# 28 transposes of the identity on TensorE ahead of the first tile, in a one-core DFT and soft mixture-of-experts kernel

## The chip, the cores and the metric

The kernel runs on one core of one Trainium2 chip. The metric is the device time in microseconds (us) of one execution. It is measured in several runs and given as their median; one further execution is recorded by the hardware profiler, and its trace is what the rows below come from. A core has five engines that run side by side and wait for each other by semaphores: TensorE (PE; its weight loads are listed apart as PEld), VectorE (DVE), ScalarE (ACT), GpSimd (POOL) and SyncE (SP), which issues the DMA transfers here.

## The reference

A real input `x` of 8 x 2496 x 256 goes through a two-dimensional Fourier transform per batch entry, of which the real part is kept. The result, as 19968 tokens of 256 values, goes through a soft mixture of experts with 8 experts of 4 slots each.

```python
X = np.fft.fft(np.fft.fft(x, axis=1), axis=2).real      # (8, 2496, 256)
X = X.reshape(8 * 2496, 256)
logits = X @ phi                                        # phi: (256, 32)
d = softmax(logits, axis=0)                             # over all tokens
slot_input = (d.T @ X).reshape(8, 4, 256)
for e in range(8):
    slot_out[e] = np.maximum(slot_input[e] @ w1[e], 0) @ w2[e]
c = softmax(logits, axis=1)                             # over the 32 slots
out = c @ slot_out.reshape(32, 256)
```

## The kernel before, in words

The batch is cut into four pairs of entries, p = 0 to 3, and each pair into five tiles of `x`, t = 0 to 4. Every tile (up to 1 MB) is loaded by SP into a ring of six buffers, in the order of the list `LD`, which also places the tables `cs0` to `cs3` and `phi`. `cs0` holds nothing but the 128 x 128 identity, named `ident`; it is the first load of all.

A hand-written list, `ORDER`, names the parts of the program. For a tile, `part_a` adds mirrored rows of `x` on DVE (lines 220 and 222), folds the columns into a tile `eo` with one addition and one subtraction (224 and 225), turns `eo` in eight transposes on PE into two banks `pt` (229) and copies them to `et` on ACT (230). `part_z` multiplies two tiles' `et` by `wphi` (244), the transformed `phi`, which is made once from `psphi` (lines 187 to 193). `part_t`, `part_b` and `part_c` finish the logits of a pair (`zt`, `a`, `lp`, `lm`, `lt`) and find maxima (`mx`, `mt`, `mall`, `mex`, `nm`) and exponentials (`d`, `dpm`). `part_e`, `part_d` and `part_u` (335, 353, 376) carry the weights back and sum the pair's tokens: `u0` reads the folded tiles `eo` of pair 0. Fifteen buffers hold `eo`, so the fold of pair 3 (225 and 224 for `eo3_0` and on) needs those that `u0` has read. After all four pairs come the experts (`part_l`, line 477, `part_v`, 497) and the output (`part_o`, 608 to 621).

`ORDER` is the order in which the program is recorded. The order in which each engine runs it is decided by the build's scheduler, which may move instructions of neighbouring parts past each other; each engine then runs its own list strictly in that order. PSUM banks come from pools: `bank1` (two buffers, `pt` and `z`), `bank` (two) and `bank3` (three, `mt`, `e`, `d`, `tok`).

Of the kernel before, what the change touches and what calls it, by code (L numbers as in the profile page):

```python
# [25 lines left out]
CT = ['sa', 'lt', 'lt', 'lt']  # L26
LATE = 'zs'
SEB = 2
DE = 2
FIRST = [0, 1]  # L30
GATE = {0: ['u', 'acc', 'acc'], 1: ['rep', 'rep', 'rep']}
# [81 lines left out]
def _build(nc, tc, xh, phih, w1h, w2h, cins, where, out, out0):  # L113
    from contextlib import ExitStack, nullcontext

    v, sc, pe = nc.vector, nc.scalar, nc.tensor
    ctx = ExitStack()
    with ctx:
# [11 lines left out]
        def se(shape, name, dt=F32):  # L130
            return sb.tile(shape, dt, name=name, tag="se", bufs=SEB)

# [6 lines left out]
        def bufs_(tag):  # L139
            return {"zs": 2, "sa": 2, "se": SEB, "lt": LT}[tag]  # L140

# [3 lines left out]
        def bank3(name, dt=F32):  # L145
            return pp.tile([128, 512], dt, name=name, tag="ps3", bufs=P3)
# [28 lines left out]
        def C(name):  # L175
            i, o, r, w = where[name]
            return cs[i][:r, o : o + w]

        ident = C("ident")


        wphi = cp.tile([128, 3, NSLOT], F32, name="wphi")
# [164 lines left out]
        def part_d(p, hf):  # L347
            if hf == 0:
                dsb[p] = se([128, 2, NKC, NSLOT], f"ds{p}")
            for k in range(2):  # L350
# [7 lines left out]
                dst = dsb[p][:, k, :, 16 * hf : 16 * hf + 16]  # L358
                (v.tensor_copy if DE >> k & 1 else sc.copy)(dst, ps[:, :320].rearrange("p (s c) -> p c s", c=NKC))  # L359

# [334 lines left out]
```

## Time and profile before

| | |
|---|---|
| median of 3 runs | 195.04 us (194.52, 195.04, 195.69) |
| the profiled execution | 194.9 us |
| its span, first to last instruction | 193.0 us |
| PE busy in the span | 169.5 us (88%) |
| DVE, ACT, POOL busy | 125.2, 111.0, 20.9 us |
| mean granted TensorE clock in the records | 0.991 |

The 1.9 us between 194.9 and 193.0 lie outside the first and the last instruction. Busy shares are averages over stages with different limits; PE's busy time is modelled from the pipelined starts of its instructions. In a row of the trace, times are us from the start of the span; `x8` is the number of instructions that a row merges; in brackets stands how long the engine sat idle before the row and what ended the wait. Lines (L229) are those of the kernel before.

### The profile page before, as it was taken

The numbers are of one execution on the slowest core, as the hardware profiler recorded it, in microseconds if no ns is written. First come the engines' busy times: TensorE is split into PE (matmuls) and PEld (weight loads), VectorE is DVE, ScalarE is ACT, GpSimd is POOL, SyncE is SP. The second block draws the span as 40 slices with busy tenths as digits, with TensorE's granted clock in tenths as the row PEclk, the third lists the DMA queues.
The fourth block names the chain that finished last, engine by engine and source line by source line (L and its number), as shares of the span: only waits on it lengthen the run. The fifth ranks groups of instructions, "written<-read, shape, count | busy, mean of one in ns | idle before, by whom it ended". The sixth has DMA issues, their size and how long they took to land.

```text
span 193.0 us, 4197 instructions
## 1 busy us (share of the span) xinstructions
PE 169.5 (88%) x1682; PEld 107.7 (56%) x1682; DVE 125.2 (65%) x227; ACT 111.0 (58%) x244; POOL 20.9 (11%) x25
## 2 busy tenths in 40 slices
PE   0389899899999989999998999999998998988930
PEld 0376576577776866576863877256535443434400
DVE  0599877999995990832267553750489776985740
ACT  2132586587966485574862842521878595774630
POOL 0000000000000000000000000550055325522000
PEclk9999999999999999999999999999999999999996
DMA  5999999999980399600860689990279999999995
GB/s 170 415 428 410 420 419 418 425 417 418 385 297 5 112 362 430 289 3 20 285 242 3 226 317 285 410 393 13 92 292 418 392 409 411 351 409 402 415 433 222
DMA packets 10706, 59.16 MB, mean 307 GB/s; under 512 B 1344, under 2 KB 1728, under 8 KB 5696
## 3 DMA queue, kind: packets, MB, share of 16 engines
q1 hardware_dynamic: 10688, 58.91, 77.1%
q8 instruction: 13, 0.21, 0.4%
q14 instruction: 5, 0.04, 0.1%
HBM read 38.46 MB, written 20.45 MB: 305 GB/s over the span
## 4 chain that ended last, share of the span: by engine, by line
PE 79%; DVE 7%; ACT 5%; DMA 3%; issue 1%; POOL 1%; SPq 0%; ACTq 0%; DVEq 0%; POOLq 0%
PE po L608 18%; PE pt L229 10%; PE z L244 8%; PE e L335 7%; PE d L353 5%; PE a L279 5%; PE u L376 4%; PE h L477 4%; PE so L497 4%; PE lT L589 3%; DMA x<-xh 3%; PE lp L297 2%; PE lm L298 2%; PE cT L530 2%; PE zt L265 2%; ACT et L230 2%
## 5 line engine op out<-in xcount | busy, mean ns | idle before, releaser
L608 PE MATMUL po<-rh,lTs 64*128 64x512 f32 x160 | 38.1, 607 | 2.2 <-ACT lTs L592 2.1
L616 DVE COPY o<-po 128x512 f32<-128x512 f32 (+1 forms) x40 | 26.7, 681 | 17.5 <-PE po L608 17.1
L229 PE MATMUL pt<-cs,eo 128*128 128x128 f32 x160 | 26.3, 301 | 7.9 <-DVE eo L224 7.8
L230 ACT COPY et<-pt 128x512 f32<-128x512 f32 x40 | 22.8, 587 | 14.6 <-PE pt L229 14.6
L616 ACT COPY o<-po 128x512 f32<-128x512 f32 x40 | 23.2, 588 | 12.1 <-PE po L608 12.1
L229 PEld LDWEIGHTS pt<-cs,eo 128*128 128x128 f32 x160 | 19.8, 153 | 14.4 <-DVE eo L224 7.8
L608 PEld LDWEIGHTS po<-rh,lTs 64*128 64x128 f32 x160 | 14.3, 186 | 17.0 <-issue 10.2
L222 DVE TENSOR_TENSOR x<-x 128x1024 f32<-128x1024 f32 x16 | 19.4, 1217 | 2.9 <-DMA x<-xh 2.9
L244 PE MATMUL z<-et,wphi 128*32 128x256 f32 (+1 forms) x288 | 16.8, 368 | 2.3 <-ACT et L230 2.3
L547 POOL TENSOR_TENSOR c<-c,cm 128x640 f32<-128x640 f32 x8 | 10.0, 1266 | 68.4 <-DVE cm L546 68.4
L320 ACT ACTIVATE d<-lt,nm 120x128 f32<-120x128 f32 x44 | 13.7, 394 | 3.6 <-DVE nm L317 3.6
L335 PE MATMUL e<-cs,dpm 120*64 120x120 f32 x176 | 14.0, 273 | 0.0
L224 DVE TENSOR_TENSOR eo<-x 128x512 f32<-128x512 f32 x20 | 13.6, 682 | 0.3
L225 DVE TENSOR_TENSOR eo<-x 128x512 f32<-128x512 f32 x20 | 13.6, 680 | 0.0
L244 PEld LDWEIGHTS z<-et,wphi 128*32 128x32 f32 x288 | 8.1, 114 | 9.2 <-ACT et L230 3.8
L335 PEld LDWEIGHTS e<-cs,dpm 120*64 120x64 f32 x176 | 11.4, 136 | 2.4 <-issue 1.8
L279 PE MATMUL a<-cs,zt 128*120 128x128 f32 x88 | 11.8, 279 | 1.0 <-DVE lt L302 0.9
L252 ACT COPY zs<-z 128x512 f32<-128x512 f32 (+1 forms) x12 | 6.2, 514 | 10.4 <-PE z L244 10.4
L557 POOL TENSOR_TENSOR c<-c,cm 128x640 f32<-128x640 f32 x8 | 10.1, 1265 | 15.0 <-DVE cm L556 11.2
L376 PE MATMUL u<-eo,ds 128*32 128x129 f32 x320 | 11.5, 275 | 0.1
L279 PEld LDWEIGHTS a<-cs,zt 128*120 128x120 f32 x88 | 10.4, 183 | 2.1 <-DVE lt L302 1.1
L353 PE MATMUL d<-e,cs 128*64 128x320 f32 x64 | 10.7, 443 | 0.5 <-ACT ds L359 0.5
(91 smaller groups left out, 217.9 us busy)
## 6 DMA issues: line engine op xcount, KB each, us to landing
x<-xh SPq DMA_DIRECT2D x16, 1024.0 KB, 12.2
out<-o SPq DMA_DIRECT2D x15, 1024.0 KB, 5.2
w<-w1h SPq DMA_DIRECT2D x6, 1024.0 KB, 8.1
w<-w2h SPq DMA_DIRECT2D x12, 512.0 KB, 6.4
x<-xh SPq DMA_DIRECT2D x4, 896.0 KB, 12.0
out<-o SPq DMA_DIRECT2D x4, 768.0 KB, 5.1
w<-w1h SPq DMA_DIRECT2D x4, 512.0 KB, 5.7
w<-w2h SPq DMA_DIRECT2D x2, 1024.0 KB, 8.1
```

What stands on the lines that cost most here:

```text
L222: v.tensor_tensor(x[:, 0:4], x[:, 0:4], x[:, 4:8], op=ALU.add)
L224: v.tensor_tensor(e[:, :, 0:128], x[:, 0:4, 0:128], x[:, 0:4, 128:256], op=ALU.add)
L229: pe.transpose(b[:, g * 128 : g * 128 + 128], e[:, g, k * 128 : k * 128 + 128], ident)
L230: sc.copy(tr[k][:, :, :, qi, :], b.rearrange("p (g h a) -> p g h a", g=4, h=2))
L244: pe.matmul(z[32 * g : 32 * g + 32, o : o + n], wphi[:, w, :], tr[k][:, g].rearrange("p h q a -> p (h q a)"), start=w != 0, stop=w != 1, t ...
L279: pe.matmul(ps[:120, i * 128 : i * 128 + 128], zt[p][:, GS * g : GS * g + GS].rearrange("p s h c -> p (s h c)"), C("wa"), start=True, stop ...
L320: sc.activation(d[:, g], L[:, g], AF.Exp, bias=nm[:, g : g + 1], scale=1.0)
L335: pe.matmul(ps[64 * k : 64 * k + 64, 120 * i : 120 * i + 120], dpm[p, hf][:, k, 3 * j + i, :], C(name), start=True, stop=True, tile_positi ...
L353: pe.matmul(ps[64 * h : 64 * h + 64, :320], C("wb")[:, 64 * k : 64 * k + 64], esb[p].rearrange("p g (s h c) -> p (g s) h c", h=2, c=NKC)[: ...
L376: last = pe.matmul(ub[32 * g : 32 * g + 32, 0:129], dsb[p][:, k, c, :], e[:, 0:129] if k == 0 else e[:, 127:256], start=cc == 0, stop=cc == 9,
L608: ins = pe.matmul(po[h], lts[p, b, t][rows], rh[0][rows].rearrange("p k d -> p (k d)"), start=True, stop=True, tile_position=(64 * h, 0),)
L616: ins = ev(ot[:np_, 2 * i : 2 * i + 2, :].rearrange("p k d -> p (k d)"), po[h][:np_])
```

## The change

After the tables are named, one tile `warm` is taken from the pool `bank3`, and PE transposes the identity into it 28 times, over its four quarters in turn. Nothing reads `warm`. The only thing that the 28 instructions need is `cs0`.

```diff
+WARM = 28
 ...
         ident = C("ident")
 
 
+        warm = bank3("warm")
+        for i in range(WARM):
+            pe.transpose(warm[:, 128 * (i % 4) : 128 * (i % 4) + 128], ident, ident)
+
+
         wphi = cp.tile([128, 3, NSLOT], F32, name="wphi")
         ps = bank("psphi")
```

Each line number behind the change is higher by 6 (L229 becomes L235). The build's scheduler also orders other instructions differently. SP's and POOL's orders are as before. PE's, DVE's and ACT's differ between the first tile and the last pair's `u`, and agree from there on, but for three swaps on DVE in the output.

The first place is the start of the program. PE's list in the kernel before (an operand's last number is a running one, and `pt0_1_0` is pair 0, tile 1, half 0):

```order
L229 MATMUL pt0_0_0_150<-cs0_70,eo0_0_140 128x128 x4
L229 MATMUL pt0_0_1_156<-cs0_70,eo0_0_140 128x128 x4
L187 MATMUL psphi_101<-phi_74,cs1_71 128x32 x4
L189 MATMUL psphi_101<-phi_74,cs1_71 1x32 x2
L229 MATMUL pt0_1_0_165<-cs0_70,eo0_1_141 128x128 x4
L229 MATMUL pt0_1_1_171<-cs0_70,eo0_1_141 128x128 x4
L244 MATMUL z0_0_178<-et0_0_1_146,wphi_100 32x256 x8
```

and with the change:

```order
L185 MATMUL warm_100<-cs0_70 128x128 x28
L235 MATMUL pt0_0_0_179<-cs0_70,eo0_0_169 128x128 x4
L235 MATMUL pt0_0_1_185<-cs0_70,eo0_0_169 128x128 x4
L193 MATMUL psphi_130<-phi_74,cs1_71 128x32 x4
L195 MATMUL psphi_130<-phi_74,cs1_71 1x32 x2
L235 MATMUL pt0_1_0_194<-cs0_70,eo0_1_170 128x128 x4
L235 MATMUL pt0_1_1_200<-cs0_70,eo0_1_170 128x128 x4
L250 MATMUL z0_0_207<-et0_0_1_175,wphi_129 32x256 x8
```

The 28 transposes stand ahead of everything else on PE; the rows behind them keep their order. DVE's list at the same place, before:

```order
L225 TENSOR_TENSOR eo0_0_140<-x0_0_76 128x4x128
L222 TENSOR_TENSOR x0_1_79<-x0_1_79 128x1024
L224 TENSOR_TENSOR eo0_1_141<-x0_1_79 128x4x128
L225 TENSOR_TENSOR eo0_1_141<-x0_1_79 128x4x128
L192 COPY wphi_100<-psphi_101 128x32 x2
L193 COPY wphi_100<-psphi_101 1x32
L222 TENSOR_TENSOR x0_2_82<-x0_2_82 128x1024
```

and with the change:

```order
L231 TENSOR_TENSOR eo0_0_169<-x0_0_76 128x4x128
L228 TENSOR_TENSOR x0_1_79<-x0_1_79 128x1024
L230 TENSOR_TENSOR eo0_1_170<-x0_1_79 128x4x128
L198 COPY wphi_129<-psphi_130 128x32 x2
L199 COPY wphi_129<-psphi_130 1x32
L231 TENSOR_TENSOR eo0_1_170<-x0_1_79 128x4x128
L228 TENSOR_TENSOR x0_2_82<-x0_2_82 128x1024
```

The copies of `psphi` now stand ahead of the second half of the fold of tile 1 (L231, L225 of before).

The second place is PE at `z2_0`, the product for the first two tiles of pair 2, some 47 us into the span of before. The kernel before:

```order
L315 MATMUL mt0_0_414<-cs0_70,mex0_0_417 120x6
L297 MATMUL lp1_0_704<-o11_685,cs2_72 120x384
L244 MATMUL z2_0_586<-et2_0_1_554,wphi_100 32x256 x8
L244 MATMUL z2_0_586<-et2_0_0_553,wphi_100 32x256 x4
L298 MATMUL lm1_0_705<-o11_685,cs2_72 120x384
L229 MATMUL pt2_2_0_605<-cs0_70,eo2_2_550 128x128 x4
L315 MATMUL mt0_1_441<-cs0_70,mex0_1_444 120x5
L229 MATMUL pt2_2_1_611<-cs0_70,eo2_2_550 128x128 x4
L265 MATMUL zt2_0_859<-cs0_70,zs2_585 128x128 x2
L229 MATMUL pt2_3_0_620<-cs0_70,eo2_3_551 128x128 x4
L335 MATMUL e0_0_0_459<-cs3_73,dpm0_0_429 64x120
L335 MATMUL e0_0_1_467<-cs3_73,dpm0_0_429 64x120
```

and with the change:

```order
L321 MATMUL mt0_1_470<-cs0_70,mex0_1_473 120x5
L303 MATMUL lp1_0_733<-o11_714,cs2_72 120x384
L304 MATMUL lm1_0_734<-o11_714,cs2_72 120x384
L250 MATMUL z2_0_615<-et2_0_1_583,wphi_129 32x256
L341 MATMUL e0_0_0_488<-cs3_73,dpm0_0_458 64x120
L341 MATMUL e0_0_1_496<-cs3_73,dpm0_0_458 64x120
L250 MATMUL z2_0_615<-et2_0_1_583,wphi_129 32x256 x7
L250 MATMUL z2_0_615<-et2_0_0_582,wphi_129 32x256 x3
L341 MATMUL e0_0_0_488<-cs3_73,dpm0_0_458 64x120 x5
L341 MATMUL e0_0_1_496<-cs3_73,dpm0_0_458 64x120 x5
L250 MATMUL z2_0_615<-et2_0_0_582,wphi_129 32x256
L235 MATMUL pt2_2_0_634<-cs0_70,eo2_2_579 128x128 x4
```

The products `e0` of pair 0, which need `dpm0_0` from DVE, stood behind the tiles 2 and 3 of pair 2; they now stand inside `z2_0`.

The third place is DVE in the same stretch, where `dpm0_0` is made. Before:

```order
L224 TENSOR_TENSOR eo2_2_550<-x2_2_119 128x4x128
L225 TENSOR_TENSOR eo2_2_550<-x2_2_119 128x4x128
L317 COPY nm0_0_420<-mt0_0_414 120x6
L314 TENSOR_SCALAR mex0_1_444<-mall_112 5x120
L224 TENSOR_TENSOR eo2_3_551<-x2_3_121 128x4x128
L225 TENSOR_TENSOR eo2_3_551<-x2_3_121 128x4x128
L222 TENSOR_TENSOR x2_4_123<-x2_4_123 128x1024
L301 TENSOR_TENSOR lt1_703<-lt1_703,lm1_0_705 120x6x64
L317 COPY nm0_1_447<-mt0_1_441 120x5
L322 TENSOR_TENSOR dpm0_0_429<-d0_0_422 120x384
L323 TENSOR_TENSOR dpm0_0_429<-d0_0_422 120x384
L220 TENSOR_TENSOR x3_0_125<-x3_0_125 128x768
```

and with the change:

```order
L320 TENSOR_SCALAR mex0_1_473<-mall_141 5x120
L230 TENSOR_TENSOR eo2_2_579<-x2_2_148 128x4x128
L231 TENSOR_TENSOR eo2_2_579<-x2_2_148 128x4x128
L328 TENSOR_TENSOR dpm0_0_458<-d0_0_451 120x384
L329 TENSOR_TENSOR dpm0_0_458<-d0_0_451 120x384
L228 TENSOR_TENSOR x2_3_150<-x2_3_150 128x1024
L323 COPY nm0_1_476<-mt0_1_470 120x5
L307 TENSOR_TENSOR lt1_732<-lt1_732,lm1_0_734 120x6x64
L228 TENSOR_TENSOR x2_4_152<-x2_4_152 128x1024
L230 TENSOR_TENSOR eo2_3_580<-x2_3_150 128x4x128
```

`dpm0_0` has moved ahead of `x2_3`, the fold of that tile and the sum of `x2_4`.

## Rows read from the trace of the kernel before

**Rows 1.** The page's busy times of the engines over the whole span, and of the chain that ended last its shares by engine.

```profile
PE 169.5 (88%) x1682; PEld 107.7 (56%) x1682; DVE 125.2 (65%) x227; ACT 111.0 (58%) x244; POOL 20.9 (11%) x25
...
PE 79%; DVE 7%; ACT 5%; DMA 3%; issue 1%; POOL 1%; SPq 0%; ACTq 0%; DVEq 0%; POOLq 0%
```

**Rows 2.** What PE waited for over the whole span (engine, line, what it waited for: us in total, times, longest us).

```profile
PE pt L229 <- DVE eo L224: 7.8, 1, 7.8
PE z L244 <- ACT et L230: 2.3, 4, 0.7
...
PE a L279 <- DVE lt L302: 0.9, 1, 0.9
```

**Rows 3.** The start of the program in order of time, all engines (start us, duration us, engine, line, operation, x count [idle before <- what ended it]).

```profile
0.74 0.39 SPq L171 DMA_DIRECT2D cs<-c  x1
...
2.60 0.65 SPq L169 DMA_DIRECT2D phi<-phih  x1
...
7.67 0.69 DVE L225 TENSOR_TENSOR eo<-x 128x512 f32<-128x512 f32 x1
...
7.81 1.97 PE L229 MATMUL pt<-cs,eo 128*128 128x128 f32 x8 [7.81 <-DVE eo L224]
...
9.28 1.22 DVE L222 TENSOR_TENSOR x<-x 128x1024 f32<-128x1024 f32 x1 [0.92 <-DMA x<-xh]
...
9.57 1.86 PE L187 MATMUL psphi<-phi,cs 128*128 128x32 f32 x8
...
11.14 0.68 DVE L225 TENSOR_TENSOR eo<-x 128x512 f32<-128x512 f32 x1
...
11.66 1.97 PE L229 MATMUL pt<-cs,eo 128*128 128x128 f32 x8
11.77 0.29 DVE L192 COPY wphi<-psphi 128x32 f32<-128x32 f32 x2
...
12.07 1.20 DVE L222 TENSOR_TENSOR x<-x 128x1024 f32<-128x1024 f32 x1
...
13.66 0.59 ACT L230 COPY et<-pt 128x512 f32<-128x512 f32 x1 [0.27 <-PE pt L229]
...
14.30 2.79 PE L244 MATMUL z<-et,wphi 128*32 128x256 f32 x24 [0.68 <-ACT et L230]
...
16.38 0.68 DVE L225 TENSOR_TENSOR eo<-x 128x512 f32<-128x512 f32 x1
...
18.78 0.66 PE L265 MATMUL zt<-cs,zs 128*128 128x128 f32 x4
18.84 0.69 DVE L225 TENSOR_TENSOR eo<-x 128x512 f32<-128x512 f32 x1
...
19.17 0.97 PEld L229 LDWEIGHTS pt<-cs,eo 128*128 128x128 f32 x8
19.27 1.11 PE L229 MATMUL pt<-cs,eo 128*128 128x128 f32 x8
...
21.06 1.50 PE L244 MATMUL z<-et,wphi 128*32 128x256 f32 x24 [0.68 <-ACT et L230]
```

**Rows 4.** DMA issues of the identity and of phi (what, queue, count, size, median us from issue to landing).

```profile
cs<-c SPq DMA_DIRECT2D x1, 64.0 KB, 1.9
phi<-phih SPq DMA_DIRECT2D x1, 32.0 KB, 6.8
```

**Rows 5.** Line 229, the transposes of the folded tiles, over the whole span (duration ns min/median/max, first and last start us).

```profile
L229 PE MATMUL pt<-cs,eo x160: 270/273/475, 7.8 to 85.2; 128*128 128x128 f32 x160
L229 PEldq EVENT_SEMAPHORE  x26: 51/51/51, 2.7 to 66.7; - x26
```

**Rows 6.** The same line's matmuls, of the first 20 us alone.

```profile
L229 PE MATMUL pt<-cs,eo x31: 272/421/475, 7.8 to 20.0; 128*128 128x128 f32 x31
```

**Rows 7.** Busy time of each engine in stretches (from:to, length, busy us of PE, PEld, DVE, ACT and POOL with counts, granted TensorE clock PEclk, DMA share, GB/s).

```profile
4.00:8.00 4.00, 0.19 (x1) 0.20 (x2) 1.90 (x3) 0.00 (x0) 0.00 (x0) 1.00 1.01 416
...
19.50:20.00 0.50, 0.50 (x7) 0.41 (x5) 0.50 (x2) 0.26 (x2) 0.00 (x0) 1.00 1.01 410
...
40.00:50.00 10.00, 9.87 (x102) 7.09 (x100) 9.72 (x17) 8.29 (x22) 0.13 (x1) 1.00 1.01 410
...
170.00:193.00 23.00, 13.41 (x62) 5.42 (x58) 11.63 (x20) 9.93 (x19) 2.53 (x2) 0.93 0.92 373
```

**Rows 8.** DVE's longer waits between 28 and 62 us, and one row of DVE (nm) and one of PE (z, which is `z2_0`) near 47 us, from the timeline (columns as in Rows 3).

```profile
28.76 1.23 DVE L222 TENSOR_TENSOR x<-x 128x1024 f32<-128x1024 f32 x1 [1.19 <-DMA x<-xh]
...
33.70 0.56 DVE L301 TENSOR_TENSOR lt<-lt,lm 120x384 f32<-120x384 f32 x1 [1.21 <-PE lm L298]
...
46.66 0.14 DVE L317 COPY nm<-mt 120x6 f32<-120x6 f32 x1
...
47.16 1.50 PE L244 MATMUL z<-et,wphi 128*32 128x256 f32 x24
...
49.60 0.55 DVE L301 TENSOR_TENSOR lt<-lt,lm 120x384 f32<-120x384 f32 x1 [0.28 <-ACT d L320]
...
59.87 0.49 DVE L359 COPY ds<-d 128x320 f32<-128x320 f32 x1 [1.05 <-PE d L353]
...
60.95 0.49 DVE L359 COPY ds<-d 128x320 f32<-128x320 f32 x1 [0.59 <-PE d L353]
...
61.93 0.27 DVE L312 TENSOR_REDUCE mall<-mt 6x3 f32<-6x120 f32 x1 [0.49 <-PE mt L310]
```

## The prediction, made before the changed kernel was run

> **What bounds the kernel now.** I read the busy times first, then PE's waits, then the start of the timeline. PE is busy 169.5 of 193.0 us and holds 79% of the chain that ended last; DVE holds 7% of it [rows 1]. PE waits for little: 7.8 us once, for the first folded tile, and then 2.3 us in four waits and 0.9 us in one in the part before the output [rows 2]. So whatever PE gets done sooner near the start can, in principle, bring the end forward, as long as the tiles reach it in time.
>
> What the reader is to see in the start is that the same work runs there at half speed. Eight transposes of `pt` take from 7.81 until `psphi` begins at 9.57, that is 0.22 us each; the eight from 19.27 take 1.11 us, and their weight loads 0.97 us for eight, 0.12 us each [rows 3]. One transpose lasts 421 ns in the median of the first 20 us and 273 ns over the whole span [rows 5, 6]. The 24 matmuls of `z` take 2.79 us at 14.30 and 1.50 us at 21.06 [rows 3]. The step lies at about 18.8 to 19.2 us. The granted-clock column does not show it: it reads 1.00, the 2.4 GHz level, in the stretch from 4 us on as well as after the step, and 0.93 only in the last one [rows 7]. I go by the durations and read them as TensorE at its lower level (1.2 GHz) until about 19 us and at 2.4 GHz from there.
>
> PE's work from 7.81 to 19 us would thus be shorter at the upper level by three groups of eight transposes, 1.76 against 0.97 us each (2.4 us), by `psphi` and by `z`. `psphi` takes from 9.57 to 11.66, 2.1 us; no row shows it at the upper level. Half would be 1.05, unchanged would be 2.1; eight of its twelve matmuls load 128 columns, as a transpose does, so I take 8 x 0.12 and something for the rest, 1.2 us. `z` takes 1.50 in place of 2.79. In all 2.4 + 0.9 + 1.3 = 4.6 us of PE work is saved, an upper bound for any gain.
>
> **The change part by part.** *The 28 transposes.* The identity is issued at 0.74 and lands 1.9 us later [rows 3, 4]; PE's first semaphore row stands at 2.7 [rows 5]. From there PE has nothing to do until 7.81 [rows 2]. 28 at 0.22 would be 6.2 us, until 8.9; 28 at 0.12 would be 3.4 us, until 6.1. If the clock rises about half-way, 14 x 0.22 + 14 x 0.12 = 4.8, until 7.5, just before the first fold is there. I take 7.5; between the bounds the first transpose of `x` is late by 0 to 1.1 us. If the cover of that wait were gone (identity as late as the first tile), they would cost 3.4 to 6.2 us. They hold one buffer of three in `bank3`, whose next user comes only with `mt` of pair 0: nothing. No DMA is added, and SP's and POOL's orders don't move.
>
> *The start at the upper clock.* The steps are bounded by what PE waits for. `phi` is issued at 2.60 and lands after 6.8 us [rows 3, 4], so `psphi` can't begin before 9.4; at 1.2 us it ends at 10.6 instead of 11.7. The copies of `psphi`, which now stand ahead of the second half of tile 1's fold, can run when DVE has done the first half (11.14) and take 0.3 us (11.77 to 12.07), the second half 0.63; DVE is again at tile 2 at 12.07, so it loses nothing [rows 3]. The last four transposes of tile 1 start at 12.1 and take about 0.55; the copy to `et` takes 0.59; `z0_0` starts near 13.35 (14.30 before), and ends at 14.85 (17.02 before). The transposes of tile 3 then wait for DVE: its fold ends at 16.38 + 0.68 = 17.06. Adding 0.55 and 0.59, `z0_1` starts at 18.3, where it started at 21.06 [rows 3]. PE is 2.8 us ahead. Even if the 28 end only at 8.9, at the upper clock `psphi` begins near 9.9 instead of 9.4, and the lead here stays, since tile 3's fold sets it.
>
> *What passes on.* DVE is the next bound: its folds begin with the landing of tiles (0.92 us idle at 9.28, 1.19 at 28.76), and in the stretch from 40 to 50 it is busy 9.72 of 10 us [rows 3, 7, 8]. PE's lead is worth only what DVE and PE stop waiting for. DVE's waits that hang on PE or ACT between 28 and 62 us are 1.21 + 0.28 + 1.05 + 0.59 + 0.49 = 3.6 us, the first 1.21 at 33.70 [rows 8]. So DVE has room for 1.2 us of the lead until it reaches pair 2 and for 3.6 us by 62 us, where it turns to the last pair. That exceeds 2.8; most of the lead can pass.
>
> *The new order* can cost. `e0`, now inside `z2_0`, needs `dpm0_0`. DVE ended the fold of `x2_2` at 46.66; without the wait of 1.21 and without the sum of `x2_3`, about 1.2 us, which now comes behind, it is there at 44.25, and `dpm0_0` adds two operations of about 0.55 (a row of `lt` of the same size takes 0.56): 45.4 [rows 8]. `z2_0` stood at 47.16; 2.8 us earlier is 44.4, or later, since `lm1_0` now stands ahead of it. So PE waits there for 0 to 1.0 us, with ACT's exponentials and all of its own list queued behind. Of this I take the middle and take off 0.5 us.
>
> *The sum*, on the profiled execution: 194.9 (193.0 span + 1.9 around it) - 2.8 + 0.5 = 192.6 us. The median before, 195.04, is 0.1 above that execution, which I leave aside.
>
> **A rule against it.** The trace bears on one doubt. Between 7.81 and 13.6 PE ran sixteen transposes and the twelve matmuls of `psphi` nearly without a pause, and the step did not come; it came after the 24 matmuls of `z` and eight more transposes [rows 3]. So no row shows that transposes alone bring it. The Trainium skill ("TensorE: Matmul & The Clock Gate", Part 4: PE-mode transpose) says that transposes do not bring TensorE to its higher clock, because they don't count as activity as other matmuls do, and gives some 275 ns for one inside a kernel. By that rule the 28 would be wasted and the time is the second rival's, 196.0 instead of 192.6. The trace has the same number, 273 ns, but as the duration at the faster level, so it does not bear out that transposes stay slow; whether they raise the clock it leaves open. The sixteen transposes that brought no step are, by themselves, reason enough for this case.
>
> **The rivals.** *First, the lead is swallowed on the way.* The first wait of DVE that PE can shorten gives 1.2 us; if the tiles of pairs 1 and 2 hold PE back after that, or the moved instructions make PE stand, 1.2 - 0.5 = 0.7 is left: 194.2 us, between 193.7 and 195.4. For it speaks DVE's 9.72 of 10 us; against it, that PE had its own long backlog (0.9 us of waiting besides `z`'s), so that other work is ready. Chance 0.18.
>
> *Second, the change doesn't do what it says:* the 28 transposes do not raise the clock. Then they last until 8.9, the first tile is turned 1.1 us late, and everything that follows at the lower level is as late: `z0_0` at 15.4. If the step comes as long after `z0_0` as before, the end is 194.9 + 1.1 = 196.0; with the order's stalls 196.5, and with DVE's slack taking half of it 195.4. It decides from the point where the clock is still low at the first row of `pt`. Chance 0.26.
>
> *Forecast:* the clock is up by the first or second tile and most of the lead stays. Its own range is 191.3 (all of DVE's 3.6) to 193.7 (1.2 alone). Chance 0.56.
>
> **How the numbers follow.** I call half a per cent, 1.0 us, the least that a measurement of this kernel can tell. The forecast's case lies beyond it almost whole (0.54 faster, 0.02 same); the first rival gives 0.03 faster, 0.13 same, 0.02 slower; the second about half same (0.12) and half slower (0.14). That makes faster 0.57, same 0.27, slower 0.16. The range goes from 191.2, beneath which a twentieth is left, to 196.1, above which a third of the second rival lies, 0.09.
>
> **What would show it.** In the profile after: a row of 28 from 2.7, ending near 7.5, in which the spacing falls from 0.22 to 0.12; the eight `pt` of the first tile in about 1.1 instead of 1.97 us; `z0_0` near 13.35 and `z0_1` near 18.3, 1.5 us each; DVE's wait for `lm` at 33.70 gone; the first fold of pair 3 two to three us earlier. The prediction is wrong if the eight `pt` at 7.8 still take 1.97 us, or if PE shows new waits for DVE of two us or more between 20 and 65 us.

## The result, and the profile after

The changed kernel takes 197.78 us (median of 20 runs, 195.02 to 198.92) beside 195.47 us for the kernel before (20 runs, 194.20 to 196.16): a ratio of 1.0066, with a 95% interval of 1.0039 to 1.0093. The ratio is below that of the medians, 1.012, because it leaves out runs over 1.5% above the fastest of their kernel, here seven of the changed kernel's 20, all at 197.97 us or more. It is slower, and outside the range of the prediction. The profiled execution took 197.18 us, its span is 195.1 us. A trace is one execution, so times of stretches in single traces are read beside the ratios. Lines of the changed kernel are those of before plus 6.

The busy times and the chain, against [rows 1]: PE has 28 instructions more and holds less of the chain.

```profile
PE 174.5 (89%) x1710; PEld 109.7 (56%) x1710; DVE 125.5 (64%) x227; ACT 111.6 (57%) x244; POOL 20.8 (11%) x25
...
PE 74%; ACT 8%; DVE 7%; DMA 4%; issue 2%; POOL 1%; SPq 1%; ACTq 0%; DVEq 0%; POOLq 0%
```

PE at the start of the changed kernel, against [rows 3] (start us, duration us, engine, line, operation, count [idle before <- what ended it]):

```profile
2.68 6.20 PE L185 MATMUL warm<-cs 128*128 128x128 f32 x28 [2.68 <-DMA cs<-c]
8.70 1.04 PE L235 MATMUL pt<-cs,eo 128*128 128x128 f32 x8
10.06 1.05 PE L193 MATMUL psphi<-phi,cs 128*128 128x32 f32 x8 [0.31 <-DMA phi<-phih]
...
14.03 1.50 PE L250 MATMUL z<-et,wphi 128*32 128x256 f32 x24 [0.68 <-ACT et L236]
```

All 28 run at the lower level, 0.22 us each; the eight transposes of the first tile, 1.97 us before, take 1.04. So transposes alone did bring the clock to its upper level, and the second rival falls. The second `z` (`z0_1`) starts at 18.96 instead of 21.06: the lead is there, 2.1 us. The next rows show where it is spent: PE around `z2_0`, which was one row of 24 matmuls in 1.50 us before [rows 8], and PE and ACT at pair 3's first tile.

```profile
47.25 0.62 PE L250 MATMUL z<-et,wphi 128*32 128x256 f32 x2
47.80 0.62 PE L341 MATMUL e<-cs,dpm 120*64 120x120 f32 x4
48.35 1.49 PE L250 MATMUL z<-et,wphi 128*32 128x256 f32 x20
49.77 1.45 PE L341 MATMUL e<-cs,dpm 120*64 120x120 f32 x20
51.14 0.62 PE L250 MATMUL z<-et,wphi 128*32 128x256 f32 x2
...
66.29 1.86 ACT L326 ACTIVATE d<-lt,nm 120x128 f32<-120x128 f32 x6
68.06 0.56 ACT L236 COPY et<-pt 128x512 f32<-128x512 f32 x1
68.67 0.66 PE L235 MATMUL pt<-cs,eo 128*128 128x128 f32 x4 [1.30 <-ACT et L236]
```

A row counts each `z` and `e` instruction twice, so the `z` that the list has as 1, 10 and 1 stand here as 2, 20 and 2. Two that stand alone take 0.55 us until the next row, a little longer than eight in a whole group (0.5). And six exponentials of pair 1 now stand on ACT ahead of a copy that PE waits 1.30 us for. Two rows of the output, and the granted clock (PEclk) in one stretch of it, first of before, then of after:

```profile
173.44 0.66 PE L589 MATMUL lT<-cs,c 128*128 128x128 f32 x4 [0.90 <-POOL c L557]
174.83 1.99 PE L608 MATMUL po<-rh,lTs 64*128 64x512 f32 x8 [0.73 <-ACT lTs L592]
```

```profile
174.35 0.66 PE L595 MATMUL lT<-cs,c 128*128 128x128 f32 x4 [1.37 <-POOL c L563]
175.74 3.62 PE L614 MATMUL po<-rh,lTs 64*128 64x512 f32 x8 [0.73 <-ACT lTs L598]
...
176.00:178.00 2.00, 2.00 (x6) 0.76 (x6) 0.28 (x1) 0.33 (x1) 0.52 (x1) 0.50 1.02 422
```

The wait ahead of the last pair is 0.47 us longer, since the scheduler put a copy of the output between DVE's `cm` and its reciprocal; behind it the clock stands at the lower level (0.50), and eight `po` take 3.62 us instead of 1.99.

DVE shows two of the signs that the prediction named, its wait for `lm` and the first fold of pair 3 (`eo3_0`), after and, last, before:

```profile
29.96 0.55 DVE L307 TENSOR_TENSOR lt<-lt,lm 120x384 f32<-120x384 f32 x1 [1.19 <-PE lm L304]
...
62.57 0.67 DVE L230 TENSOR_TENSOR eo<-x 128x512 f32<-128x512 f32 x1
```

```profile
63.45 0.67 DVE L224 TENSOR_TENSOR eo<-x 128x512 f32<-128x512 f32 x1
```

Eleven profiled executions are laid side by side at four marks (single executions; the ratios are of many): the start of `z0_1`, of the first `u` (pair 0), of the first and of the last `po`.

| kernel | z0_1 at | z0_1 to u | u to po | po to last po | span | ratio to before |
|---|---|---|---|---|---|---|
| before | 21.06 | 40.76 | 74.24 | 48.4 | 193.0 | |
| after | 18.96 | 42.65 | 74.89 | 50.5 | 195.1 | 1.0066 |
| w16 | 20.07 | 41.19 | 74.23 | 48.4 | 192.1 | 0.9978 |
| w22 | 19.86 | 41.16 | 74.25 | 48.4 | 192.0 | 0.9993 |
| old28 | 18.28 | 42.37 | 74.23 | 48.4 | 191.5 | 0.9979 |
| new0 | 21.58 | 42.65 | 75.49 | 50.5 | 198.2 | 1.0248 |
| after_z | 18.41 | 41.43 | 74.89 | 48.9 | 191.7 | 0.9978 |
| after_zt | 18.37 | 41.43 | 74.91 | 48.4 | 191.3 | 0.9936 |
| after_zte | 18.63 | 41.43 | 73.94 | 48.4 | 190.6 | 0.9882 |
| after_zte2 | 18.88 | 41.43 | 74.01 | 48.4 | 190.9 | 0.9888 |
| new0_zte | 20.67 | 41.43 | 73.94 | 48.4 | 193.0 | 1.0049 |

The ledger of the change is the difference of the first two lines: -2.1 at `z0_1`, +1.9 to `u`, +0.65 to `po`, +2.1 to the last `po` (0.47 of the longer wait, 1.63 of the eight slow `po`). That is +2.55 us at the last `po`; the transfers behind it take 8.1 instead of 8.55 us, so the span is 2.1 us longer. The kernels below tell what each term is. The 1.63 us are this execution's, and executions differ: of the changed kernel's 20, four took 195.0 to 195.3 us at a mean granted clock of 0.987 or 0.988, and eleven 197.7 us or more at 0.977 or less.

### The profile page after: what moved, and what is told of

The parts are those of the page before. It is cut to its first block, busy times and chain, and to the rows that moved or that the text cites. A ratio compares the mean times of both kernels' runs of the same rounds, so it can differ in the third digit from the quotient of the medians.

```text
span 195.1 us, 4251 instructions
## 1 busy us (share of the span) xinstructions
PE 174.5 (89%) x1710; PEld 109.7 (56%) x1710; DVE 125.5 (64%) x227; ACT 111.6 (57%) x244; POOL 20.8 (11%) x25
## 4 chain that ended last, share of the span: by engine, by line
PE 74%; ACT 8%; DVE 7%; DMA 4%; issue 2%; POOL 1%; SPq 1%; ACTq 0%; DVEq 0%; POOLq 0%
PE po L614 19%; PE z L250 7%; PE e L341 6%; PE pt L235 6%; PE a L285 6%; PE u L382 6%; PE d L359 5%; DMA x<-xh 4%; PE h L483 4%; PE so L503 4%; ACT et L236 3%; PE lT L595 3%; PE lm L304 2%; PE cT L536 2%; PE lp L303 2%; DVE x L228 2%
## 5 line engine op out<-in xcount | busy, mean ns | idle before, releaser
L614 PE MATMUL po<-rh,lTs 64*128 64x512 f32 x160 | 39.8, 629 | 2.2 <-ACT lTs L598 2.1
L235 PE MATMUL pt<-cs,eo 128*128 128x128 f32 x160 | 24.6, 279 | 2.6 <-ACT et L236 1.3
L235 PEld LDWEIGHTS pt<-cs,eo 128*128 128x128 f32 x160 | 17.9, 141 | 9.3 <-issue 4.2
L326 ACT ACTIVATE d<-lt,nm 120x128 f32<-120x128 f32 x44 | 13.7, 391 | 3.1 <-DVE nm L323 3.1
L230 DVE TENSOR_TENSOR eo<-x 128x512 f32<-128x512 f32 x20 | 13.6, 680 | 0.3
L231 DVE TENSOR_TENSOR eo<-x 128x512 f32<-128x512 f32 x20 | 13.5, 677 | 0.0
L341 PE MATMUL e<-cs,dpm 120*64 120x120 f32 x176 | 13.0, 273 | 0.0
L365 DVE COPY ds<-d 128x320 f32<-128x320 f32 x8 | 3.9, 488 | 13.6 <-PE d L359 13.6
L382 PE MATMUL u<-eo,ds 128*32 128x129 f32 x320 | 12.0, 276 | 0.1
L341 PEld LDWEIGHTS e<-cs,dpm 120*64 120x64 f32 x176 | 10.5, 136 | 2.7 <-issue 0.7
```

The lines of the kernel that those rows point to most:

```text
L230: v.tensor_tensor(e[:, :, 0:128], x[:, 0:4, 0:128], x[:, 0:4, 128:256], op=ALU.add)
L231: v.tensor_tensor(e[:, :, 128:256], x[:, 0:4, 0:128], x[:, 0:4, 128:256], op=ALU.subtract)
L235: pe.transpose(b[:, g * 128 : g * 128 + 128], e[:, g, k * 128 : k * 128 + 128], ident)
L326: sc.activation(d[:, g], L[:, g], AF.Exp, bias=nm[:, g : g + 1], scale=1.0)
L341: pe.matmul(ps[64 * k : 64 * k + 64, 120 * i : 120 * i + 120], dpm[p, hf][:, k, 3 * j + i, :], C(name), start=True, stop=True, tile_positi ...
L382: last = pe.matmul(ub[32 * g : 32 * g + 32, 0:129], dsb[p][:, k, c, :], e[:, 0:129] if k == 0 else e[:, 127:256], start=cc == 0, stop=cc == 9,
```

## The experiments

**Fewer transposes in the old order.** With 16 the scheduler leaves every list as before; with 22 only the copies of `psphi` move.

```diff
-WARM = 28
+WARM = 16   # w16;  w22: WARM = 22
```

At that point I took the output's copies for the cause, so two more runs moved them alone.

> 16 transposes: 3.5 us at 0.22 each, until 6.2, then 1.6 us of pause until the first fold. The order on all engines is exactly that of the kernel before. If 16 are enough for the clock and the pause does not undo it, as with 22 (A: 194.3 to 195.3; B: 192.7 to 193.5); if not, the first eight transposes take 1.97 us, the step comes where it came before or a little sooner, and the time is before's within 0.3%.

> 22 transposes in place of 28. With this count the scheduler leaves the order of the kernel before on every engine, but for the copies of psphi, which stand ahead of the second half of tile 1's fold as in the changed kernel. So this is the warm start without the new order, in the middle and in the output. Theory A (the lead is swallowed by DVE and the landing of x, whatever the order; the loss sits in the output): z0_1 starts 1.5 to 2.5 us earlier than 21.06, the first fold of pair 3 (63.45 before) less than 1 us earlier, PE's pause in the output stays 0.9 us and the clock stays up there; 194.3 to 195.3 us, 0 to 0.5% below before. Rival B (the new order of pairs 1 to 3 swallows the lead): with the old order the lead is kept, first fold of pair 3 at 61.5 or sooner, 192.7 to 193.5 us. Rival C (28 were needed, 22 don't raise the clock): the eight transposes of the first tile take 1.97 us again and the time is before's.

w16: 0.9978 (0.9941 to 1.0015), w22: 0.9993 (0.9958 to 1.0028). Neither can be told from before. In the traces both reach `po` 0.6 to 0.8 us ahead. In both the clock went up and came back. In w22 PE paused 0.55, 0.78, 0.55, 0.26 and 0.68 us for DVE, `phi` and ACT between 7 and 13.7 us, and `z0_0` ran slowly again, at 2.79 us (second row: PEclk from 14 to 16 us). In w16 the first tile took 1.26 us, behind a pause of 1.61 us, and `psphi` was slow again, 1.89 us instead of 1.05 in after (last two rows).

```profile
13.63 2.79 PE L250 MATMUL z<-et,wphi 128*32 128x256 f32 x24 [0.68 <-ACT et L236]
...
14.00:16.00 2.00, 2.00 (x24) 0.79 (x16) 1.97 (x4) 0.00 (x0) 0.00 (x0) 0.50 1.00 421
```

```profile
7.70 1.26 PE L235 MATMUL pt<-cs,eo 128*128 128x128 f32 x8 [1.61 <-DVE eo L230]
9.63 1.89 PE L193 MATMUL psphi<-phi,cs 128*128 128x32 f32 x8 [0.67 <-DMA phi<-phih]
```

**The output's copies alone.** after_pin is the changed kernel with DVE's three copies behind the reciprocals again (and a fourth, which before too has ahead); before_swap is the kernel before with the three ahead.

```diff
+                    with tc.issue_after(recip[0]) if h and recip else nullcontext():    # after_pin
                         ins = ev(ot[...], po[h][:np_])
 ...
+SPLIT = ((2, 0), (3, 0), (3, 1))      # before_swap: their reciprocals are recorded behind the copies
```

> The changed kernel with one thing forced: each DVE copy of an output bank goes out behind the last reciprocal recorded ahead of it, so that the three swaps of the output are undone (and a fourth of the same kind that before had too). All else is the changed kernel, the new order of pairs 1 to 3 too. Theory A: PE's pause ahead of the output of pair 3 goes from 1.37 back to 0.9 us and the granted clock stays 1.00 there; the eight matmuls behind it take 1.99 instead of 3.62 us; 197.2 - 0.45 - 1.63 = 195.1 us, equal to before within 0.4%. Rival D (the clock falls in the output whatever the length of that pause, as a late effect of the warm start): still 3.6 us for the eight matmuls, 196.7 to 197.2 us.

> The kernel before, no warm-up, with only the three swaps of DVE in the output made by hand: the reciprocals of c2, c3 (first half) and c3 (second half) are issued behind the copy of an output bank that they stood ahead of. Theory A: PE's pause there becomes 1.3 to 1.4 us, the clock falls to the lower level for some 3.5 us in most executions; 195.5 + 0.45 + 1.6 = 197.5 us, 1% slower than before. Rival D: no fall, 195.5 to 196.0 us.

after_pin: 1.0089 (1.0043 to 1.0135), before_swap: 1.0001 (0.9964 to 1.0037). The copies alone are not the cause. The drop of the clock in the output does not follow from them alone either: in after_pin's trace the wait is 0.90 us again, and yet the clock drops there (0.50 from 178 to 180 us) as well as at the start. In before_swap's trace (an execution of 196.70 us, the longest of its twelve) the wait is 1.37 us and the clock drops too. First after_pin, then before_swap:

```profile
176.69 3.01 PE L616 MATMUL po<-rh,lTs 64*128 64x512 f32 x8 [0.73 <-ACT lTs L600]
```

```profile
175.45 3.50 PE L614 MATMUL po<-rh,lTs 64*128 64x512 f32 x8 [0.73 <-ACT lTs L598]
```

Over all traces without added transposes in the output, the drop stands in four of the eight with a wait of 1.36 or 1.37 us (after, before_swap, new0, new0_d; not light0, light28, old_new28, after_z) and in one of the ten with 0.90 or 0.91 us (after_pin). So the longer wait may make it likelier; that many single executions don't show it.

**The order and the row apart.** For all kernels from here on but light0 the lists of PE, DVE and ACT are written out, as edges that set the order and add no wait. new0 has the changed order without the row, old28 the old order with it.

```diff
+IN_ORDER = {'PE': [(0, 8), ...], 'DVE': [...], 'Activation': [...]}    # stretches of the recorded order
+        own = [own[n + k] for a, b in runs for k in range(a, b)]
+        for a, b in zip(own, own[1:]):
+            tc.add_manual_dep(b, a.name, DependencyInfo(DependencyClass.NoSync, DependencyReason.DATA), ...)
```

> The kernel before, with no transposes of the identity, but with the instructions of PE, DVE and ACT listed one behind the other in the order in which they stand in the changed kernel. Nothing else differs, so whatever the early row does to the clock or to the first tile is absent here and only the order is left. Order theory (the order of pairs 1 to 3 is what costs): about as slow as the changed kernel, 1.007 to 1.015 of the kernel before (some 196.5 us beside 195), with the exponentials of pair 1 again between two copies of a transposed tile of pair 3 and PE waiting over 1 us for ACT there. Early-row theory (the order is free and the transposes themselves, by what the clock does after them, cost the time): within 0.3% of the kernel before. Should it be over 1.015, the lead of 2 us of the changed kernel is worth something after all, and the order hides it.

> The changed kernel with its 28 transposes, but with PE, DVE and ACT in the order of the kernel before. Order theory: 0.995 to 1.000 of the kernel before, with the first tile's transposes at 8.7 us as in the changed kernel, x's later tiles and DVE swallowing the 2 us by about 60 us, and the output started 0.3 to 1 us ahead. Early-row theory: 1.005 or more, as the changed kernel. My forecast ahead of the first run, that a lead of 2 us passes on to the end, would need 0.990 or less; what 16 and 22 transposes in the old order gave (0.998 and 0.999) speaks against it.

new0: 1.0248 (1.0200 to 1.0295), old28: 0.9979 (0.9947 to 1.0012). The order costs, and more than its theory said; with the row the same order is at 1.0066, so the row repays 1.8% of before there (each against its own runs of before). old28 has the whole lead forecast at `z0_1` (18.28 forecast 18.3) and loses 1.6 us of the 2.8 by `u`, at one place: pair 1's second tile lands too late for PE's list.

```profile
23.54 1.23 DVE L228 TENSOR_TENSOR x<-x 128x1024 f32<-128x1024 f32 x1 [2.04 <-DMA x<-xh]
...
25.63 0.63 PE L235 MATMUL pt<-cs,eo 128*128 128x128 f32 x4 [1.53 <-DVE eo L230]
```

Behind it nothing more is lost: from the first `a` of pair 0 to `u` the old order takes 34.55 us in before, w16, w22 and old28 alike. In the changed order PE has other work at that place, and `z0_1` to `u` is 42.65 us with the row and without: its lead passes whole. PE's waits of over 0.15 us between the two marks add up to 1.27 us in both traces. new0 also corrects a reading of mine. DVE stands there 4.43 us for pair 0's logits, and PE loses nothing by it:

```profile
32.57 0.55 DVE L301 TENSOR_TENSOR lt<-lt,lm 120x384 f32<-120x384 f32 x1 [4.43 <-PE lm L298]
```

In after DVE waits 1.19 us for those logits and is then busy without a pause (from:to, length, busy us of PE, PEld, DVE, ACT and POOL, PEclk, DMA share, GB/s), and PE needs the same 42.65 us between the marks:

```profile
40.00:50.00 10.00, 9.81 (x78) 6.59 (x78) 10.00 (x18) 8.05 (x22) 0.13 (x1) 1.00 1.00 405
```

**x and DVE lightened.** Both kernels load half of x and leave out DVE's first sum of each tile, so their output is another one. The edit, and in light28 the row and light0's lists besides:

```diff
-                r0, n = (0, 7) if t == 0 else (7 + 8 * (t - 1), 8)
+                r0, n = (0, 4) if t == 0 else (7 + 8 * (t - 1), 4)
-                v.tensor_tensor(x[:, 0:4], x[:, 0:4], x[:, 4:8], op=ALU.add)
```

> The kernel before with half of the load of x and DVE's first sum of each tile (the mirrored rows) left out: only 4 of a tile's rows are loaded and used, so its numbers are other ones. It is the base for the next kernel, with the same order of what is left. About 14 us of DVE's work and 9.5 MB of transfers are gone. If PE alone bounded the stretch from 25 to 62 us, it would win what the DVE and transfer waits there add up to (some 5 us), to 190; if little hangs on them, 193 to 194.

> The same lightened kernel (half of x and DVE's first sums left out) with the 28 transposes ahead, in exactly the order of the lightened kernel without them. Theory that x's later tiles and DVE swallow the early lead: with both lightened the lead of about 2 us at the first fold should reach the output, so 1.5 to 2.5 us under the lightened kernel without transposes. Rival (the lead is lost elsewhere, to the clock falling back once PE waits for data in the first 20 us, or to the order of waits behind it): 0 to 0.7 us under it.

light0: 195.94 us, 1.0067 (1.0027 to 1.0106), so the lightening itself won nothing (its scheduled order is another one). light28: 194.17 us, 0.9991 (0.9954 to 1.0027), 1.8 us under light0, as was expected; the two profiled executions are 0.73 us apart. In the traces light28 leads by 0.77 us at `z0_1` (light0's first tile came early, at 6.24), at `u` (52.69 and 53.46) and at `po`: with x landing in time light0's order passes this smaller lead on whole.

**One engine's list put back.** new0_d is new0 with DVE's 34 instructions from pair 0's logits to pair 3 in the old order.

```diff
-    'DVE': changed order
+    'DVE': changed[:27] + old[27:61] + changed[61:]
```

> No transposes of the identity; PE and ACT in the changed kernel's order, and DVE too, but for its 34 instructions from the first logit fold of pair 0 up to pair 3's first sum, which stand as in the kernel before. The changed order without the row took 1.025 of the kernel before, and in its trace DVE stood 4.43 us for the logits of pair 0 (lm) with three sums and folds of pair 1 queued behind them. Theory that this queue is the price of the order: that wait falls to about 1 us and the time to 1.005 to 1.012. Rival (the price is in the order of PE and ACT, the wait only shows it): 1.018 or more, with the lost time in other waits.

1.0671 (1.0620 to 1.0722): a miss. Now PE waits for DVE, 2.45 us once, 1.22 us once, and 2.57 us for ACT. The price is over the rival's 1.018, but the run doesn't prove the rival: it shows that the three lists fit each other, and that one alone can't be judged.

**The two parts of the order apart**, and **more transposes in the output**.

```diff
-    'PE': changed order                 'DVE': ...              'Activation': ...
+    'PE': changed[:344] + old[344:]     changed[:74] + old[74:]  changed[:70] + old[70:]   # new_old28
+    'PE': old[:344] + changed[344:]     ...                                              # old_new28
+        if j == 0 and p == 3: 6 x pe.transpose(ps[...], ident, ident)          # old28_fill, ahead of lT
+        if j == 0 and p in (1, 2, 3): 5 x pe.transpose(more[...], ident, ident)  # behind lT
```

> 28 transposes; PE, DVE and ACT in the changed order up to about 61 us (PE's first u of pair 0) and in the order before from there on, the output included. It cuts the cost of the changed order in two. By the traces of the two orders with 28 transposes: the first part ends 1.0 us later than in the old order (u of pair 0 at 61.6 instead of 60.6), and nothing more is lost behind it: 194.5 to 195, 1.002 to 1.006 of the kernel before. If the cost sits in the later part, it is as the old order with 28 transposes (0.998).

> 28 transposes; the order before up to about 61 us and the changed order from there on, with the three copies of the output ahead of the reciprocals. By the traces: u of pair 0 at 60.6 as in the old order, 0.6 us lost between 61 and 110 us (pair 1's exponentials between two copies of a transposed tile, PE waiting 1.3 us for ACT), 0.5 us at the last pair's output, and more often the drop of the clock there (1.5 us): 195 to 196.5, 1.003 to 1.011. If all of the cost sits in the first part: 0.998.

> 28 transposes, all in the order before, and 21 more transposes of the identity in the output part, where PE waits: 6 ahead of the last pair's first transposes (0.91 us of wait for POOL) and 5 between the first transposes and the products of pairs 1, 2 and 3 (0.7 us of wait for ACT). Theory that the slower third of the runs is the granted clock falling to 0.50 in the output after these waits: all runs at 193.3 to 194.2, median 0.4 to 0.8 us under the kernel before (0.996 to 0.998 or less, upper bound below 1), and the clock in the trace unbroken. Rival (the slower runs come from elsewhere, or the output is bound by its transfers): a quarter to a third of the runs still at 194.9 or more, median as without the 21.

new_old28: 1.0112 (1.0066 to 1.0159), old_new28: 1.0069 (1.0031 to 1.0107): both parts cost. new_old28 is above its band because the seam added a wait of PE for ACT's `ds` (1.60 us at 62.78). old_new28 loses 0.45 us from `u` to `po` and has the longer wait in the output (1.36 us); its trace also lost the clock at the start (`z0_0` in 2.79 us, `z0_1` at 19.45). old28_fill: 0.9992 (0.9966 to 1.0018). All 12 runs lie within 193.91 to 194.39, as the clock theory had it, where old28's spread from 193.40 to 195.83; but the median is no better. So the spread of this order fits the drop in the output (old28's one trace has none), but the filling does not pay. Its trace shows no loss there; `phi` and the second tile landed later, which gave it `z0_1` at 19.06.

**The changed order mended.** after_z puts the 12 instructions of `z2_0` together, after_zt the output's copies back as well, after_zte pair 1's exponentials behind the copy as well, after_ztef adds the 21 transposes.

```diff
-  PE:  z2_0 x1, e0_0 x1, e0_1 x1, z2_0 x10, e0_0 x5, e0_1 x5, z2_0 x1
+  PE:  z2_0 x12, e0_0 x6, e0_1 x6                                          # after_z
-  DVE: o2_3, reciprocal cm3_0, ...    +  DVE: reciprocal cm3_0, o2_3, ...  # after_zt (three places)
-  ACT: exponentials d1_0, et3_0_1     +  ACT: et3_0_1, exponentials d1_0   # after_zte (d1_1 too)
```

> The changed kernel, but on PE the 12 matmuls of z of pair 2's first part (z2_0) stand together ahead of e of pair 0, where the changed order has 1 of them, 2 of e, 10 of z, 10 of e, 1 of z. In the trace of the changed kernel these z and e take 4.44 us from 47.25, in the old order with 28 transposes the same z 1.43 and e 1.99, since four z run side by side when they stand together. Theory that this cut is the first part's price: z and e in about 3.4 us, u of pair 0 at 60.6 to 60.8, the time 0.8 to 1.0 us under the changed kernel's: 1.001 to 1.003 of the kernel before. Rival (DVE sets the pace there, so PE only waits elsewhere): z in 1.4 us, but u of pair 0 still at 61.3 or later, and 1.006 as the changed kernel.

> As the run with z2_0 together, and with the three copies of the output behind the reciprocals again, as in the kernel before. Expected: the wait ahead of the last pair's transposes 0.91 instead of 1.37 us, so 0.4 to 0.5 us less, and fewer runs in which the clock drops in the output: 0.996 to 1.001. If the copies' place is free, as undoing it alone in the changed kernel and doing it alone in the kernel before had it: as the run without.

> As the run before (z2_0 together, output's copies in the old place), and on ACT the exponentials of pair 1 stand behind the copy of the second half of pair 3's transposed tile, both times, instead of ahead of it. Expected if ACT's queue there costs what PE waits for it (1.30 and 0.79 us, of which 0.86 is PE's wait for DVE in the old order): the wait of 1.30 gone, 0.4 to 0.6 us less up to the output's start. Rival: what is queued behind the exponentials (zt of pair 2, the logits of pair 1) is late instead, and nothing is won.

> As the run before, with 21 more transposes of the identity where PE waits in the output. Expected: no run in the slower cluster and the clock unbroken from 9 us to the end, so all runs at 193 to 194.3 and a median of 0.992 to 0.997 of the kernel before, if the mends have given the lead back; 0.998 to 1.000, as the old order with 28 and 21, if x's arrival and DVE swallow the lead whatever the order.

after_z: 0.9978 (0.9951 to 1.0005), after_zt: 0.9936 (0.9904 to 0.9968), after_zte: 0.9882 (0.9853 to 0.9911). All three are below what was expected. Neighbouring intervals overlap; those of after, after_z and after_zte don't. Each mend shows in its own column of the table: 42.65 to 41.43, 48.9 to 48.4 (50.5 with the drop of the clock), 74.9 to 73.9. `z` and `e` of after_z take 2.9 us where the changed kernel takes 4.4; PE then waits 0.45 us for the copy of `z`, and of the 1.5 us some 1.1 are left, nearly all of the column's 1.2:

```profile
46.69 1.50 PE L250 MATMUL z<-et,wphi 128*32 128x256 f32 x24
48.13 1.50 PE L341 MATMUL e<-cs,dpm 120*64 120x120 f32 x24
```

In after_zte a wait of 1.17 us for `zt` stands where the wait of 1.30 us was, so that one hardly shrank; the other, of 0.79 us at 80.89 in after_z, is gone (first after_zte, then after_z).

```profile
67.42 0.80 PE L304 MATMUL lm<-o,cs 120*120 120x320 f32 x2 [1.17 <-ACT zt L276]
```

```profile
80.89 1.50 PE L250 MATMUL z<-et,wphi 128*32 128x256 f32 x24 [0.79 <-ACT et L236]
```

after_ztef: 0.9938 (0.9919 to 0.9957), five runs within 194.17 to 194.49. Its trace lost the clock at the start (`z0_0` in 2.53 us, `z0_1` at 20.43, 1.8 us behind after_zte); whether all five runs did, and so why its whole level is above after_zte, is not settled.

**The row in the mended order.**

```diff
-        for i in range(WARM):                      # new0_zte: after_zte without the row
-            pe.transpose(warm[...], ident, ident)  # after_zte2: after_zte again
```

> The changed order with its three places mended (z2_0 together, the output's copies and pair 1's exponentials in the other places), without the row of 28. Theory that the row's lead is what the changed order needs: DVE stands again over 4 us for pair 0's logits at 32 us, u of pair 0 at 62.5 to 63.5, and the time is 1.003 to 1.010 of the kernel before, 1.5 to 2% over the same order with the row. Rival (the mended order is simply the better one): 0.985 to 0.995, within 0.5% of the same order with the row.

> The mended kernel with the row once more, for the spread: 0.985 to 0.992 of the kernel before, as in its first six runs (0.988), runs at 192.4 to 194.0.

new0_zte: 195.43 us, 1.0049 (1.0017 to 1.0080); after_zte2: 192.81 us, 0.9888 (0.9854 to 0.9922). On the same chip the row is worth 2.6 us of the median in this order. In the traces, whose executions took 194.88 and 192.86 us, after_zte2 leads by 1.8 us at `z0_1` and at `u`, and by 1.7 at `po`; the columns between are the same within 0.1 us. after_zte is 1.1 to 1.2% (2.1 to 2.3 us) under before, and the changed kernel was 0.7% above it.

## Why the prediction was wrong

- **The row and the clock: right, with a smaller number.** The 28 ended at 8.88, the upper bound (8.9), not at 7.5; the clock did not rise half-way. The doubt that transposes raise no clock is settled by the rows at 2.68 and 8.70: nothing but transposes ran on PE before, and the next eight took 1.04 us. The Trainium skill ("TensorE: Matmul & The Clock Gate", Part 4: PE-mode transpose) says the contrary; the measurement decides. What the forecast took for granted, that the level stays once reached, did not hold in five of the 14 traces with a row (w16, w22, after_pin, old_new28, after_ztef), where `z0_0` took 2.24 us or more.
- **The start: right in kind.** `z0_0` at 14.03 (forecast 13.35) and `z0_1` at 18.96 (18.3). The second tile landed at 9.75 instead of 9.28, which the sum did not allow for; in old28, where it landed at 9.06, they are 13.07 and 18.28. Lead 2.1 instead of 2.8 us.
- **What passes on: right for the changed order, by a wrong reason.** I held DVE for the next bound and let the lead pass by DVE's waits for PE. `z0_1` to `u` is 42.65 with DVE idle 4.43 us in it (new0) and with DVE busy 10.00 of 10 us from 40 to 50 (after). So PE's own list set the pace in that order, and DVE's busy share said nothing. The wait for `lm`, forecast gone, is still 1.19 us (at 29.96), and the first fold of pair 3 is at 62.57, 0.9 us earlier than before (63.45), not two to three. In the old order the first rival was right: 1.6 of 2.8 us swallowed on the way, by x's landing.
- **The new order: the step that failed.** I took off 0.5 us, for PE waiting 0 to 1.0 us for `dpm0_0` inside `z2_0`. The place was right, the kind and the size were not. PE did not wait there; the cut group itself took 1.2 us more (42.65 against 41.43 when mended). Beside it the order cost 0.7 us more to `u` (41.43 in the mended order with the row and without, 40.76 in before). No run took that apart; in the traces PE's waits of over 0.15 us on the way are 0.76 us longer there (1.73 against 0.97). It cost 0.65 us from `u` to `po` (1.0 by the mend of ACT's list), and 0.47 us in the output. Neither ACT's list nor DVE's in the output was in the forecast. In all 3.0 us of order instead of 0.5. The prediction's two signs of being wrong, a slow first tile and new waits for DVE of two us or more, did not show: they looked at the clock and at DVE, and the loss was in PE's own list and behind ACT.
- **The clock later on: not foreseen.** The forecast kept it at the upper level once reached. The profiled execution of after lost 1.6 us to its drop in the output (3.62 - 1.99). Why it drops in some executions and not in others, and whether the change makes it more frequent, stays open. With the lead of 2.1 in place of 2.8, 3.0 of order in place of 0.5 and this 1.6, the sum is 194.9 - 2.1 + 3.0 + 1.6 = 197.4; the profiled execution took 197.18.
- **The sign.** Once the three places are mended, the kernel takes 193.1 and 192.8 us on two chips, 1.1 to 1.2% under before. That this is what was forecast for the change (192.6 us, 1.2%) is in part luck: it is another order, and its ACT list gains more than the changed order had lost there (`u` to `po` is 73.9 in it, 74.24 in before). The forecast had the row's lead about right (2.8 us; 1.8 to 2.8 at `z0_1` between traces of one order with and without it, 0.8 in the lightened pair) and the reshuffled order wrong by a factor of six.

What stays open: why after_pin, with the output mended alone, was no faster than after. Its trace has the clock low at the start (`z0_1` at 20.37) and in the output, but a trace is one execution.

## What to carry over

Where a scheduler decides the lists, a change at the start is two changes: price the new lists apart, by walking through each engine's rows for groups that were whole and are now cut, and for work moved ahead of a copy that PE waits for. A lead is worth what the engine's own list lets through, so compare the time between fixed marks in both kernels, not busy shares. And write the order out to keep the old lists with the new code, or the new lists without it: new0, old28, new0_zte and after_zte told cause from cause here.

## What the runs showed of the hardware

- Transposes of the identity alone brought TensorE from the lower to the upper level of its clock (28 at 0.22 us each from 2.68, then eight in 1.04 us at 8.70).
- The clock falls back in the middle of a busy stretch: in w22 after pauses of at most 0.8 us between 8 and 13.6 us, in after behind waits of 1.37 and 0.73 us, in after_pin behind 0.90 and 0.73. The same pairs of waits stand in other traces without a drop, the first in after_z and light28, the second in before and old28.
- A matmul of `z` fills 32 columns of the array, and the group places four at four column positions. In the single matmul records of before and old28 four begin within 21 ns, and the next four 0.2 us later; at 47.25 and 47.49 in the changed kernel they begin one by one. The Trainium skill ("TensorE: Matmul & The Clock Gate", Part 3: Packing small matmuls — row/col tiling) says that small matmuls at different column positions run at the same time. The trace agrees, by the 21 ns. What the runs add is the price of cutting such a group into 1, 10 and 1: 1.2 us.
